# Three blocks of mm1 by seven products instead of four, in a fused retention and gelu kernel

## The chip, the core and the metric

The kernel runs on one core of one Trainium2 chip. A core has five engines that run their own instruction streams: PE (TensorE, matmuls; its weight loads are shown apart as PEld), DVE (VectorE), ACT (ScalarE), POOL (GpSimd) and SP (SyncE, which here only issues DMAs). They meet through semaphores. The metric is the device time of one execution in microseconds, taken several times. Durations are read from one further, profiled execution.

## The reference: what is computed

Retention with a decay, and then a feed-forward layer:

```
scores = q @ k^T / 8                      # 8 batches, 8 heads, 576 tokens, 64 per head
ret    = scores * gamma[h]**(i - j)       # for i >= j, else 0
x      = (ret @ v), heads side by side    # 4608 tokens x 512
h      = x @ w_in                         # mm1: 512 -> 2048
g      = gelu(h), tanh form
out    = g @ w_out                        # mm2: 2048 -> 512
```

All inputs and the output are float32. The kernel computes in float16 with float32 sums.

## The kernel before

**Units and blocks.** The tokens of a batch are cut into units of 128 (the fifth of a batch has 64), 40 units in all. Retention works by units: within a unit by masked scores, from earlier units by a decayed state. Its output goes transposed into `xT` (line 421), a ring of three blocks. The feed-forward layer works by blocks of 512 tokens, 0 to 8. mm1 gives h transposed in PSUM, gelu (ACT) moves it into `gT` (a ring of two blocks), and mm2 reads it from there. PSUM banks for mm1 and for mm2 are two each (`take`, line 426).

**Seven products.** A product of 2 x 2 blocks can be had with seven products of blocks instead of eight, with sums of blocks before and after (Winograd's form of Strassen's scheme). The kernel does so in two places.

- mm2 of 16 pairs of tiles of 128 tokens (blocks 1 to 7 whole, and half of 0 and of 8): `sum_a` (line 874) makes sums of gT, `sum_b` (852) sums of w_out once, `product` (892) is one of seven products of 8 matmuls of 256 columns, `assemble` (924) adds the parts on DVE or copies them on DVE or ACT.
- mm1 of the last blocks of tokens: `sum_w` (960) makes sums of w_in once, `sum_x` (977) four sums of a block's xT on DVE, `product_h` (984) is one of seven products of 4 matmuls for each of four groups of chunks, `part_h` (1007) copies three parts out of PSUM and adds three on DVE, `gelu_h` (1016) is the gelu of what comes of it. The sums of w_in lie in pages 9 to 20 of the 21 input pages, so from the first `sum_w` on, and for units from `LATE` (line 181) on, loads use nine pages only (`page`, line 185).

**The list of steps.** The order of all instructions is written out: `ORDER` (line 17) is a string of steps made beforehand, and the loop at line 1087 calls one small function for each. Every engine runs its part of the list in that order, so what stands on one engine behind a waiting instruction waits too. A step's letter, its function and its engine:

| step | does | engine |
|---|---|---|
| L,u,n | loads q, k or v (n = 0, 1, 2) of unit u; units 0, 2, 5, 7 are loaded two at once ("wide", 512 KB) | SP's queue |
| I,g,by / J,g,by | loads one of eight pieces of w_in / w_out; by g: POOL's queue with the cast in the transfer; by p: SP's queue as float32 into a staging slot (`load_w`, line 253) | POOL or SP |
| i,g,eng / j,g,eng | casts a staged piece; does nothing for a piece that came by g (`cast_w`, 261) | DVE, ACT or POOL |
| q, k, v | scale or cast a unit's input to float16 (lines 439 to 493) | DVE, ACT, POOL |
| t, y / D | transpose q and k: by PE and a copy / by a DMA | PE, then DVE or ACT / SP |
| X, Y, R, B | retention's matmuls of wide units / of others | PE |
| m, a, o, z, x | mask, state, its decay, its float16 copy, output to xT | DVE, ACT, POOL |
| N,t,fc,half | mm1 of block t: two chunks of 128 features, 256 tokens (8 matmuls of 256 columns, line 790) | PE |
| M,t,fc[,part] | mm1: one chunk, 512 tokens (4 matmuls of 512), or with a part four chunks, 128 tokens (16 of 128) | PE |
| F, G | gelu after N, M (line 798) | ACT |
| U / s / A / l / f | sums of w_in / sums of xT / one of the products of mm1 / copy or addition / gelu | DVE / DVE / PE / ACT, DVE / ACT |
| O, e | plain mm2, a quarter of the sum for 128 tokens (line 816); its result | PE; DVE, ACT |
| T / H / W / V | sums of w_out / sums of gT / one of the products of mm2 (line 904) / parts and results (all DVE sums and additions show as line 850) | DVE / DVE / PE / DVE, ACT |
| P, E, Q | mm2 of the last 128 tokens by columns (line 1031), result, store | PE; DVE, ACT; SP |
| S | store | SP |
| K,n | n dummy matmuls of 512 columns (line 1046) | PE |
| Z, g, c, b, w | constants: zeroed state buffers, rows of decays, mask, tables, the gelu table | POOL, DVE, ACT |

mm2 of earlier blocks and mm1 of later ones are interleaved on PE, with retention's small matmuls between them.

Of the kernel before, what the change touches and what calls it, by code (L numbers as in the profile page):

```python
# [17 lines left out]
Z,0,g L,4,1 L,0,2 L,0,1 Z,1,v g,g Z,3,v c k,0,a L,0,0 b I,6,g L,2,0 v,0,v K,4 K,4 K,4 K,4 t,0,k,h  # L18
y,0,k,v q,0,g Z,5,v X,0 I,7,g K,4 K,1 t,0,q,h I,2,g L,2,1 q,2 y,0,q,v a,0,1,g z,0,1,a I,3,g a,1,1
K,4,o K,3,o Y,0,1 L,2,2 Z,2,g L,4,0 m,0,1 k,2,a K,4 K,2 Y,0,0 m,0,0 o,1,1 t,2,k,h L,5,0 t,2,q,h  # L20
y,2,k,a R,0 L,5,1 I,1,g y,2,q,v x,1 x,0 L,4,2 I,0,g z,1,1,g K,4 Y,2,0 L,5,2 L,7,0 k,4,v v,2,v
t,4,k,o N,0,12,0 I,4,g N,0,14,0 w y,4,k,a X,2 m,2,0 a,2,1 F,0,12,0 F,0,14,0 L,7,1 a,3,1 Y,2,1 I,5,g
z,2,1,g m,2,1 N,0,6,0 N,0,4,0 F,0,4,0 q,4,g F,0,6,0 R,2 x,3 t,4,q,o x,2 N,0,0,0 N,0,2,0 q,5 y,4,q,a
v,4,g B,4,-1 F,0,0,0 m,4 Z,4,g J,1,g N,0,4,1 F,0,2,0 t,5,q,o M,0,9 y,5,q,v k,5,v v,5,v J,0,g F,0,4,1
N,0,0,1 G,0,9 J,2,g M,0,8 L,7,2 t,5,k,o z,3,1,v F,0,0,1 N,0,12,1 q,7,g G,0,8 y,5,k,a J,3,g N,0,14,1
Y,5,0 J,4,g k,7,g X,5 F,0,12,1 F,0,14,1 M,0,10 m,5,0 N,0,2,1 a,5,1,g J,7,g t,7,q,o L,9,0 a,6,1
G,0,10 B,-1,4 z,5,1,v Y,5,1 J,5,g m,5,1 M,0,11 F,0,2,1 N,0,6,1 t,7,k,o x,4 J,6,g y,7,k,v y,7,q,a R,5
O,0,4 O,0,0 o,6,1 F,0,6,1 Y,7,0 x,5 x,6 G,0,11 N,1,4,0 N,1,0,0 F,1,4,0 F,1,0,0 O,0,1 O,0,5 L,14,1
L,9,1 N,1,14,0 F,1,14,0 v,7,g H,0,1,5,v m,7,0 U,1,0 N,1,2,0 F,1,2,0 Y,7,1 X,7 L,9,2 a,7,1 z,7,1,a
N,1,10,0 O,0,6 N,1,6,0 F,1,6,0 m,7,1 q,9,g k,9,g a,8,1 z,6,1,v O,0,7 U,2,0 L,11,0 T,1,0,v e,0,1,v  # L30
H,0,1,2,v T,1,1,v R,7 v,9,g L,13,0 j,2,g F,1,10,0 D,9 T,2,1,v x,7 N,1,12,0 x,8 q,11 L,10,0 H,0,1,4,v
W,0,1,1 O,0,2 L,14,2 F,1,12,0 q,10,g L,10,1 N,1,12,1 L,11,1 F,1,12,1 T,2,0,v O,0,3 T,3,1,v B,9,-1
e,0,0,a T,4,0,v k,10,v V,0,1,0,v L,10,2 L,14,0 D,10 N,1,8,0 q,13 N,1,0,1 L,12,0 W,0,1,5 F,1,8,0
F,1,0,1 N,1,2,1 T,4,1,v N,1,14,1 F,1,2,1 L,11,2 k,11,g F,1,14,1 D,11 L,13,1 W,0,1,6 m,9 i,2,g
V,0,1,1,a N,1,8,1 T,3,0,v v,10,v j,4,g L,16,0 N,1,10,1 F,1,8,1 W,0,1,7 z,8,1,v B,10,9 V,0,1,3,a
L,12,1 x,9 m,10 V,0,1,4 N,1,4,1 W,0,1,4 F,1,10,1 a,10,0,g N,1,6,1 a,10,1 z,10,1,a W,0,1,3 v,11,g
z,10,0,v H,1,0,5,v B,11,10 V,0,1,5,v L,12,2 q,12 m,11 F,1,6,1 W,0,1,2 q,14 k,13,g a,11,0 F,1,4,1
W,1,0,1 x,10 N,2,10,0 L,15,0 V,1,0,0,a k,12,g N,2,14,0 H,1,0,2,v F,2,10,0 F,2,14,0 H,1,1,5,v V,0,1,6
V,0,1,2 v,12,v W,1,0,6 H,1,1,2,v L,16,1 j,3,v D,12 N,2,8,0 L,15,2 N,2,4,0 V,1,0,1,v L,13,2 D,13
L,15,1 a,11,1 o,11,1 z,11,0,a W,1,1,1 F,2,8,0 W,1,0,7 F,2,4,0 v,14,g B,12,11 V,1,1,0,v H,1,0,4,v  # L40
v,15,v i,5,a S,0,1 q,15,g a,12,0 z,11,1,a v,13,g i,0,a L,19,1 N,2,0,0 U,1,1 m,12 W,1,1,6 x,11 L,18,0
# [88 lines left out]
def kernel(  # L130
# [11 lines left out]
    B, H, S, D = q.shape  # L142
# [12 lines left out]
    G = 64  # L155
# [25 lines left out]
    LATE = 26  # L181
# [595 lines left out]
    gTs, h = {}, {}  # L777
# [341 lines left out]
```

## Time and profile before

| | |
|---|---|
| time, median of 3 runs | 295.02 us (294.54 to 295.3) |
| the profiled execution | 295.5 us |
| its span in the profile | 293.8 us |
| granted TensorE clock | 1.00 |
| PE, PEld, DVE, ACT, POOL busy | 280.0, 233.0, 225.7, 166.6, 95.7 us |
| matmuls of plain mm1 (L790) | 608, 79.0 us |
| matmuls of mm1 by seven products (L1001) | 192 + 128 + 64 + 64 |
| matmuls of mm2 by seven products (L904) | 384 + 256 + 128 + 128 |
| HBM read, written | 36.70 MB, 9.44 MB |

A busy PE is the time in which some matmul is in its pipeline; a single matmul of 256 columns is shown as 273 ns long, though the next one starts earlier. What one costs in a row of them is seen from the length of a group in the chain of waits. Lines in the profile name the helper that issues an instruction, so DVE's sums and additions share line 850 and are told apart by their tiles: `pages` and `hc` are those of mm1 by seven products, `ssum` and `tsum` those of mm2.

### The profile page before, as it was taken

How to read it: one execution, taken by the hardware profiler on the slowest of the kernel's cores; microseconds unless marked ns; L12 is line 12 of the kernel's file. 1: busy time of each engine (PE TensorE's matmuls, PEld its weight loads, DVE VectorE, ACT ScalarE, POOL GpSimd, SP SyncE). 2: the span in 40 equal slices, each digit the busy share in tenths (PEclk: the TensorE clock that was granted, in tenths of full speed). 3: DMA queues.
4: the chain of work that ended last, by engine and by line, in shares of the span. 5: the costliest groups of instructions: out<-in, count | busy, mean ns of one | idle time of the engine just before them, and what ended most of it. 6: DMA issues, size and time to landing. Idle time of an engine off the chain costs nothing.

```text
span 293.8 us, 9639 instructions
## 1 busy us (share of the span) xinstructions
PE 280.0 (95%) x4042; PEld 233.0 (79%) x4042; DVE 225.7 (77%) x446; ACT 166.6 (57%) x325; POOL 95.7 (33%) x157
## 2 busy tenths in 40 slices
PE   7697999999999999999999899999999999999995
PEld 2366767788888888888888778878887788888874
DVE  6684874986976798748758798899988989985841
ACT  2464763456655534656457558578576697655510
POOL 7841791202531321434643534644313301000000
PEclk9999999999999999999999999999999999999999
DMA  6999999949989979999998979997948430110112
GB/s 159 312 247 212 310 203 207 186 94 225 169 207 233 198 168 196 222 206 159 248 206 196 184 163 197 197 188 193 181 87 187 109 126 2 38 74 36 74 71 108
DMA packets 136428, 49.77 MB, mean 169 GB/s; under 512 B 118209, under 2 KB 130881, under 8 KB 136385
## 3 DMA queue, kind: packets, MB, share of 16 engines
q1 hardware_dynamic: 132032, 44.97, 70.6%
q0 software_dynamic: 4352, 4.20, 8.5%
q8 instruction: 31, 0.51, 0.8%
q14 instruction: 13, 0.10, 0.1%
HBM read 36.70 MB, written 9.44 MB: 157 GB/s over the span
## 4 chain that ended last, share of the span: by engine, by line
PE 77%; DVE 11%; DMA 5%; issue 2%; ACT 1%; SPq 1%; POOL 1%; DVEq 0%; POOLq 0%; ACTq 0%
PE bank L904 29%; PE bank L790 21%; PE bank L1001 14%; PE bank L816 4%; DMA w_in_sb<-in_moe_w_in_dram 3%; DVE ssum L850 2%; DVE pages L850 2%; PE sk L574 2%; PE x L550 2%; DMA pages<-in_q_dram 2%; PE sk L584 1%; PE x L595 1%; PE bank L1031 1%; DVE sz L764 1%; DVE hc L850 1%
## 5 line engine op out<-in xcount | busy, mean ns | idle before, releaser
L790 PE MATMUL bank<-xT,w_in_sb 128*128 128x256 f16 (+1 forms) x608 | 79.0, 279 | 1.8 <-ACT xT L607 0.9
L798 ACT ACTIVATE gT<-bank 128x512 f16<-128x512 f32 x80 | 47.0, 597 | 39.5 <-PE bank L790 39.2
L790 PEld LDWEIGHTS <-w_in_sb 128*128 128x128 f16 x608 | 57.5, 98 | 13.2 <-DMA w_in_sb<-in_moe_w_in_dram 2.5
L904 PEld LDWEIGHTS <-ssum 128*128 128x128 f16 x512 | 49.8, 98 | 6.8 <-DVE ssum L850 0.9
L904 PE MATMUL bank<-tsum,ssum 128*128 128x256 f16 x384 | 49.3, 273 | 0.3 <-DVE ssum L850 0.3
L904 PEld LDWEIGHTS <-gT 128*128 128x128 f16 x384 | 37.0, 98 | 4.4
L441 POOL TENSOR_TENSOR v<-pages,dec 128x512 f16<-128x512 f32 (+1 forms) x24 | 24.2, 1010 | 48.5 <-DMA pages<-in_v_dram 26.6
L286 POOL CAST sz<-s 64x256 f16<-64x256 f32 x36 | 17.3, 479 | 62.1 <-DVE s L746 51.6
L904 PE MATMUL bank<-w_out_sb,gT 128*128 128x256 f16 x256 | 32.9, 273 | 0.0
L1001 PEld LDWEIGHTS <-pages 128*128 128x128 f16 x256 | 24.2, 98 | 7.1 <-issue 2.9
L1001 PE MATMUL bank<-pages 128*128 128x256 f16 x192 | 27.9, 273 | 1.9 <-DVE pages L850 1.3
L722 DVE TENSOR_TENSOR ret<-sk,mask 128x512 f16<-128x512 f32 (+1 forms) x32 | 19.8, 618 | 9.8 <-PE sk L584 5.2
L850 DVE TENSOR_TENSOR ost<-u,bank 128x256 f32<-128x256 f32 x48 | 19.4, 416 | 9.5 <-PE bank L904 9.3
L850 DVE TENSOR_TENSOR ssum<-gT,ssum 128x1024 f16<-128x1024 f16 x32 | 24.0, 754 | 0.1
L284 ACT COPY hc<-bank 128x512 f32<-128x512 f32 x27 | 15.8, 586 | 14.1 <-PE bank L1001 13.8
L850 DVE TENSOR_TENSOR ssum<-gT 128x2048 f16<-128x2048 f16 (+1 forms) x20 | 21.3, 1063 | 2.7 <-ACT gT L798 2.1
L850 DVE TENSOR_TENSOR hc<-hc,bank 128x512 f32<-128x512 f32 x29 | 19.8, 684 | 4.0 <-PE bank L1001 3.8
L1001 PEld LDWEIGHTS <-w_in_sb 128*128 128x128 f16 x192 | 18.6, 98 | 2.9 <-DVE pages L850 0.6
L441 POOL TENSOR_TENSOR qk<-pages,dec 128x512 f16<-128x512 f32 (+1 forms) x16 | 17.1, 1070 | 9.7 <-DMA pages<-in_q_dram 4.8
L746 DVE TENSOR_TENSOR s<-s,sk 128x256 f32<-128x256 f32 x36 | 15.0, 416 | 5.8 <-PE sk L584 4.5
L1001 PE MATMUL bank<-xT,w_in_sb 128*128 128x256 f16 x128 | 19.2, 273 | 0.0
L1019 ACT ACTIVATE gT<-hc 128x512 f16<-128x512 f32 x29 | 17.8, 630 | 2.0 <-DVE hc L850 2.0
(117 smaller groups left out, 445.9 us busy)
## 6 DMA issues: line engine op xcount, KB each, us to landing
out_dram<-ost SPq DMA_DIRECT2D x35, 256.0 KB, 2.6
pages<-in_q_dram SPq DMA_DIRECT2D x32, 256.0 KB, 5.1
pages<-in_k_dram SPq DMA_DIRECT2D x24, 256.0 KB, 4.4
pages<-in_v_dram SPq DMA_DIRECT2D x24, 256.0 KB, 4.4
pages<-in_v_dram SPq DMA_DIRECT2D x4, 512.0 KB, 12.5
pages<-in_k_dram SPq DMA_DIRECT2D x4, 512.0 KB, 6.9
w_in_sb<-in_moe_w_in_dram POOLq DMA_DIRECT2D x8, 256.0 KB, 10.2
w_out_sb<-in_moe_w_out_dram POOLq DMA_DIRECT2D x8, 256.0 KB, 7.9
```

The source lines that it names most:

```text
L284: nc.scalar.copy(out=o, in_=i)
L286: (nc.vector if eng == "v" else nc.gpsimd).tensor_copy(out=o, in_=i)
L441: eng.tensor_tensor(out=out, in0=pages[:, page_of[s["u"], i], 0:n], in1=dec[:, i // 2, s["j"], 0:n].unsqueeze(2).to_broadcast([128, n, D]) ...
L722: nc.vector.tensor_tensor(out=ret[:, :, 0:n], in0=now["two"][:, :, 0, 0:n], in1=mask.unsqueeze(1).unsqueeze(1).to_broadcast([128, 2, n, G] ...
L746: nc.vector.tensor_tensor(out=s32, in0=state[0], in1=kv, op=ALU.add)
L790: nc.tensor.matmul(hps[:, i, :], w_in_sb[:, ct, 128 * (fc + i) : 128 * (fc + i) + 128], xT[:, ct, TB * t % XR + lo : TB * t % XR + hi], st ...
L798: nc.scalar.activation(out=gTs[t][:, fc : fc + TB // (hi - lo), lo:hi], in_=h.pop((t, fc, lo)), func=AF.Gelu_apprx_tanh, bias=0.0, scale=1.0,)
L816: nc.tensor.matmul(ops[t, tcc], gTs[t][:, ft, 128 * tcc : 128 * tcc + 128], w_out_sb[:, ft, :], start=(ft == 0), stop=(ft == NFC - 1),)
L850: (nc.vector if eng == "v" else nc.gpsimd).tensor_tensor(out=out, in0=a, in1=b, op=op)
L904: nc.tensor.matmul(p["ps", bank][:, HN * col : HN * col + HN], a[:, k], b[:, k], start=(k == 0 and fresh), stop=(k == HK - 1), skip_group_ ...
L1001: nc.tensor.matmul(p["ps", bank][:, n], w[:, c, 128 * n : 128 * n + 128], x[:, c], start=(n == 0 and c == 0 and i in (1, 2, 5)), stop=(c = ...
L1019: nc.scalar.activation(out=gTs[t][:, f : f + 2, o : o + 256], in_=p["ps", 0] if i == 0 else p["c", i], func=AF.Gelu_apprx_tanh, bias=0.0, ...
```

## The change

Only the string `ORDER` and one number are changed. The steps that differ in number or kind:

| step | before | after |
|---|---|---|
| blocks of mm1 by seven products | 5, 6, 7, 8 | 6, 7, 8 |
| A (products of mm1) | 112 | 84 |
| s (sums of xT) | 16 | 12 |
| l (copies and additions) | 96 | 72 |
| f (gelu after these) | 64 | 48 |
| N (8 matmuls of 256) | 72 | 64 |
| M of 4 matmuls of 512 / of 16 matmuls of 128 | 8 / 0 | 24 / 8 |
| F, G (gelu after these) | 72, 8 | 64, 32 |
| W (products of mm2), pairs | 112, 16 | 112, 16 |
| H (sums of gT; step 5 makes two sums at once) | 52 | 55 |
| K (dummy matmuls) | 38 | 42 |
| pieces of w_in by POOL's queue / by SP's | 8 / 0 | 7 / 1 |
| all steps | 1369 | 1336 |

Nearly every step stands at another place than before, and many of q, k, v, z, V, l and y are done by another engine: q on DVE 18 to 11 and on POOL 18 to 25, z on DVE 20 to 11, on POOL 22 to 27 and on ACT 14 to 18. `g` (rows of decays) goes from POOL to DVE. The head of the list, where w_in and w_out are loaded, and the entry into seven products:

```diff
-Z,0,g L,4,1 L,0,2 L,0,1 Z,1,v g,g Z,3,v c k,0,a L,0,0 b I,6,g L,2,0 v,0,v K,4 K,4 K,4 K,4 t,0,k,h
-y,0,k,v q,0,g Z,5,v X,0 I,7,g K,4 K,1 t,0,q,h I,2,g L,2,1 q,2 y,0,q,v a,0,1,g z,0,1,a I,3,g a,1,1
...
-v,4,g B,4,-1 F,0,0,0 m,4 Z,4,g J,1,g N,0,4,1 F,0,2,0 t,5,q,o M,0,9 y,5,q,v k,5,v v,5,v J,0,g F,0,4,1
...
-L,29,0 L,28,1 o,26,1 x,26 s,5,1 F,4,10,1 V,3,0,2,a F,4,14,1 W,3,1,2 A,5,0,1 s,5,2 W,4,0,1 L,29,1
...
+L,0,1 Z,1,v Z,5,v g Z,4,g L,0,2 L,0,0 k,0,a K,4 K,3 t,0,k,o v,0,v b q,0 I,0,g K,3 X,0 a,0,1,g a,1,1
+L,2,0 K,4 K,4 K,3 t,0,q,h y,0,k,a I,1,g c I,6,g L,2,1 z,0,1,g y,0,q,a L,2,2 q,2 L,4,0 K,4 K,1 Y,0,1
+m,0,1 L,4,1 L,5,0 K,4 K,2 Y,0,0 L,5,1 w t,2,q,h y,2,q,a k,2,v K,4 K,1 t,2,k,o m,0,0 o,1,1 y,2,k,v
+R,0 x,0 K,2 Y,2,0 M,0,0,0 x,1 Z,2,g v,2,v I,2,p Z,3,v Z,0,g I,7,g z,1,1,a q,4,g I,3,g G,0,0,0 K,1
+X,2 m,2,0 a,2,1 N,0,12,0 a,3,1 k,4,a k,5,g I,4,g t,4,k,o Y,2,1 z,2,1,a L,5,2 t,4,q,o L,7,0 N,0,14,0
+F,0,12,0 F,0,14,0 I,5,g m,2,1 R,2 y,4,k,a M,0,0,1 y,4,q,a x,2 B,4,-1 M,0,0,2 t,5,k,o x,3 q,5 L,7,1
+i,2,v m,4 t,5,q,o L,4,2 G,0,0,1 G,0,0,2 M,0,4 M,0,5 v,5,g y,5,k,v L,7,2 J,1,g q,7,g G,0,4 M,0,6
+G,0,5 N,0,12,1 y,5,q,a X,5 J,0,g Y,5,0 z,3,1,v G,0,6 m,5,0 J,3,g F,0,12,1 M,0,7 L,10,1 k,7,v G,0,7
...
+F,5,12,0 z,25,1,g a,26,1 D,27 L,31,0 N,5,0,0 H,4,0,2,v V,3,1,6,v m,26 x,25 F,5,0,0 L,30,0 v,27,g
...
+k,34,v o,31,1 m,31 s,6,3 v,32,g V,4,1,5,a W,4,1,3 A,6,0,1 V,4,1,2,a z,30,1,g L,36,1 z,31,1,g s,6,2
+W,5,0,1 L,35,1 H,5,1,3,v H,5,1,1,v l,6,0,0,a A,6,0,6 V,5,0,0,a V,4,1,6,v L,37,1 A,6,0,2 l,6,0,1,a
...
-    LATE = 26
+    LATE = 31
```

The first sum of w_in (U), from which on nine pages serve for loads, stands near unit 14's loads before and near unit 23's casts after.

More of the change, by code (lines that the diff above doesn't have):

```diff
@@ new lines @@
+W,2,0,7 H,2,1,3,v z,16,0,g G,2,8,3 a,16,1 N,3,8,0 m,16 N,3,12,0 H,2,1,1,v F,3,8,0 D,19 W,2,0,2
+B,17,16 V,2,0,3,v F,3,12,0 H,2,0,4,v o,16,1 N,3,10,0 H,2,1,2,v W,2,0,4 a,17,0 x,16 V,2,0,2,a
+z,16,1,g D,18 V,2,0,4,v L,20,1 a,17,1 m,17 L,22,1 F,3,10,0 N,3,6,0 W,2,0,3 L,21,1 z,17,0,a v,18,v
+H,2,1,4,v F,3,6,0 N,3,4,0 N,3,2,0 z,17,1,g L,21,2 V,2,0,6,v V,2,0,5,v k,21,v B,18,17 L,20,0 F,3,4,0
+F,3,2,0 W,2,1,1 a,18,0 m,18 N,3,14,0 V,2,1,0,v L,19,2 a,18,1 F,3,14,0 L,22,0 W,2,1,2 x,17 z,18,0,g
+q,22,g q,20 W,2,1,6 L,24,0 L,22,2 S,1,2 N,3,8,1 k,22,v V,2,1,1,v S,1,3 L,20,2 N,3,12,1 B,19,18
@@ new lines @@
+W,2,1,7 z,18,1,v k,20,v q,21,g W,2,1,5 F,3,8,1 D,20 N,3,6,1 L,23,0 V,2,1,3,a F,3,12,1 x,18 F,3,6,1
+W,2,1,4 N,3,0,1 H,3,0,5,v v,20,g v,19,g m,19 B,20,19 v,22,g N,3,14,1 H,3,0,2,v V,2,1,5,v V,2,1,4,v
+v,21,g W,2,1,3 W,3,0,1 F,3,0,1 V,2,1,2,a a,20,0 D,21 F,3,14,1 k,23,v x,19 U,1,0 S,2,1 N,3,4,1
+z,20,0,a m,20 N,3,2,1 V,2,1,6,v F,3,4,1 D,22 a,20,1 L,24,1 F,3,2,1 B,21,20 U,3,0 j,0,g a,21,0
+N,3,10,1 L,25,1 W,3,1,1 L,23,2 z,20,1,g q,24,g N,4,2,0 x,20 m,21 z,21,0,g V,3,0,0,a k,24,g L,27,0
+L,24,2 a,21,1 v,23,g L,27,1 W,3,0,6 F,3,10,1 N,4,12,0 F,4,2,0 S,2,0 H,3,1,5,v q,23,g U,1,1 L,26,2
@@ new lines @@
+l,7,0,2,a q,37,g A,7,0,2 m,36 k,39,a D,37 l,7,0,3,v W,6,0,5 a,36,1 o,36,1 S,5,0 f,6,3,3 A,7,0,4
+A,7,0,5 f,7,0,0 f,7,0,1 L,38,2 z,36,1,a W,6,0,6 A,7,1,1 l,7,0,4,v A,7,0,3 D,38 l,7,1,0,a l,7,0,5,v
+S,5,1 v,38,g B,37,36 A,7,1,6 V,6,0,1,a j,4,g D,39 A,7,1,2 v,39,g l,7,1,1,a W,6,0,7 m,37 a,37,0
+l,7,1,3,v a,37,1 A,7,1,7 x,36 V,6,0,3,v V,6,0,4,v l,7,1,2,a H,6,0,4,v A,7,1,5 f,7,1,1 z,37,0,g
+B,38,37 m,38 S,5,3 f,7,0,3 A,7,1,4 f,7,1,0 f,7,0,2 W,6,0,4 A,7,2,1 V,6,0,5,a l,7,1,4,v A,7,1,3
+a,38,0 H,6,1,5,v W,6,0,3 l,7,2,0,a z,38,0,g V,6,0,2,a S,5,2 A,7,2,6 l,7,1,5,v W,6,1,1 A,7,2,2
@@ new lines @@
+H,6,1,2,v l,7,2,1,a V,6,1,0,a A,7,2,7 W,6,1,6 f,7,1,3 l,7,2,3,v A,7,2,5 x,37 l,7,2,2,v A,7,2,4
+V,6,0,6,v l,7,2,4,v V,6,1,1,a f,7,2,1 a,38,1 f,7,2,0 f,7,2,2 W,6,1,7 A,7,2,3 l,7,2,5,v A,7,3,1
+W,6,1,2 i,4,a A,7,3,2 l,7,3,0,a A,7,3,6 f,7,1,2 V,6,1,3,v l,7,3,3,v W,6,1,5 l,7,3,1,v z,37,1,a
+z,38,1,g B,39,38 H,6,1,4,v V,6,1,2,a A,7,3,7 m,39 W,6,1,4 x,38 f,7,2,3 B,-1,39 l,7,3,2,v A,7,3,5
+f,7,3,1 V,6,1,4,v l,7,3,4,v A,7,3,4 x,39 f,7,3,0 V,6,1,5,a s,8,1 W,6,1,3 s,8,3 A,7,3,3 A,8,0,1 s,8,2
+l,8,0,0,a W,7,0,1 l,7,3,5,v S,6,1 V,7,0,0,a V,6,1,6,v A,8,0,6 l,8,0,1,a H,7,0,5,v s,8,4 A,8,0,2
@@ new lines @@
+W,7,0,2 A,8,0,7 H,7,0,2,v W,7,0,6 j,7,v f,7,3,3 l,8,0,3,v f,7,3,2 S,6,2 l,8,0,2,a V,7,0,1,a
+H,7,1,5,v A,8,0,4 A,8,0,5 f,8,0,0 l,8,0,4,v W,7,0,7 A,8,1,1 A,8,0,3 W,7,0,5 l,8,0,5,v l,8,1,0,a
+V,7,0,3,v A,8,1,6 A,8,1,2 l,8,1,3,v f,8,0,1 H,7,0,4,v W,7,0,4 f,8,0,3 l,8,1,1,a A,8,1,7 A,8,1,5
+V,7,0,5,a l,8,1,2,a A,8,1,4 V,7,0,4,v W,7,0,3 H,7,1,2,v S,6,3 S,6,0 f,8,1,0 l,8,1,4,v A,8,1,3
+A,8,2,1 f,8,0,2 l,8,2,0,a V,7,0,2,a f,8,1,1 W,7,1,1 l,8,1,5,v A,8,2,2 V,7,1,0,v A,8,2,6 W,7,1,6
+l,8,2,1,a l,8,2,3,v A,8,2,7 V,7,0,6,v A,8,2,5 l,8,2,2,v V,7,1,1,a f,8,1,2 W,7,1,7 H,8,0,3,v A,8,2,4
@@ L126 @@
+Q,2
 """
```

167 lines of the change are left out of this document (63 added, 104 removed).

## The prediction

> **What bounds the kernel now.** I read the stretches of the span first, then the PE's waits, then the chain of waits at the start, then the DMA issues. The page's head and four stretches:
>
> ```profile
> PE 280.0 (95%) x4042; PEld 233.0 (79%) x4042; DVE 225.7 (77%) x446; ACT 166.6 (57%) x325; POOL 95.7 (33%) x157
> ...
> 45.00:165.00 120.00, 119.74 (x1886) 102.85 (x1885) 89.85 (x170) 65.25 (x131) 39.12 (x50) 1.00 1.00 196
> 165.00:200.00 35.00, 33.21 (x505) 28.74 (x503) 31.48 (x60) 23.53 (x47) 16.18 (x24) 1.00 0.88 184
> 200.00:240.00 40.00, 38.62 (x557) 34.04 (x555) 37.46 (x72) 27.82 (x57) 10.55 (x15) 1.00 0.67 144
> 240.00:280.00 40.00, 39.47 (x442) 34.75 (x440) 31.18 (x61) 25.92 (x50) 0.79 (x2) 1.00 0.13 50
> ```
>
> Columns: stretch, length, then busy us of PE, PEld, DVE, ACT, POOL, the granted clock, DMA share, GB/s. From 45 to 165 us the PE idles 0.26 us: nothing but its work counts there. From 165, where blocks 5 to 8 take mm1 by seven products, it idles 1.79, 1.38 and 0.53 = 3.7 us, and DVE is 90 and 94% busy in the first two stretches. The PE's waits from 160 to 290 us are nearly all for DVE:
>
> ```profile
> PE bank L1001 <- DVE pages L850: 1.6, 3, 0.8
> PE bank L1001 <- DVE hc L850: 0.8, 2, 0.7
> PE bank L1001 <- ACT hc L284: 0.5, 2, 0.3
> ```
>
> Before 45 us transfers set the pace: the DMA share is 1.03 from 0 to 30 us and 1.20 from 30 to 45, and the PE fills its waits with dummy products K.
>
> **The change, part by part.** The tally used below is the list of steps, each step's instructions times the mean of their row. DVE instructions overlap a little, so its sums (246 us before) stand 9% above the busy time (225.7); I use differences and ratios only.
>
> *Products.* The chain of waits has the price of a matmul of 256 columns:
>
> ```profile
> 59.12 0.86 PE bank L816 x4
> ...
> 159.62 1.75 PE bank L790 x16
> ```
>
> 1.75 / 16 = 0.109 us. A plain block has 16 steps N of 8 such matmuls, 128; a block by seven products 4 groups x 7 x 4 = 112. Block 5 goes from 112 to 128: **+16 x 0.109 = +1.75 us**, on the engine that sets the end, with no cover. M steps of 512 columns (4 matmuls, as in the four of L816 above, 0.86) cost what an N costs. Eight M steps now take 128 columns (16 matmuls). Nearest row: in the tail L1031 does 16 of 256 and 16 of 128 columns in 2.80 us, so 16 of 128 take at most 2.80 - 1.75 = 1.05 with the pipeline's end in it; 0.87 to 1.05 against 0.87, for eight 0 to +1.4. I take 0, since most of the difference is that end.
>
> *What leaves DVE.* Block 5 no longer needs 4 sums s of xT (4 x 0.60 = 2.4), 12 additions l (12 x 0.684 = 8.2) nor 12 copies l (mostly ACT's, 12 x 0.586 = 7.0). By choice of engine in the new list z loses 8.8 on DVE and q 4.5, k and v gain 3.2. In all the tally gives DVE -17.7, ACT -8.4, POOL +9.3 us. None of that is the end by itself; it counts only through the PE's 3.7 us of waits. Those split so. The two waits where block 5's sums come in (168.66 us: 0.77, and 171.09: 0.37, both for "DVE pages L850") are the price of entering seven products; block 6 now enters first, so I keep them. The other 0.65 of the stretch 165 to 200 goes with block 5. For the 1.38 and 0.53 of blocks 6 to 8, compare equal work: from the first sum of block 6 to the first of block 8 the old list has 59.7 us of DVE steps to 57.0 of PE, the new one 55.8 to 56.5. DVE is relieved by 6.5% there, not more, because nearly all that left is block 5's own. I take 0.55 of these 1.9 as gone. **-1.2 us**, between -0.65 (only block 5's own) and -3.5 (all waits).
>
> At the entry, one rule speaks against the change:
>
> ```profile
> 167.34 1.26 DVE L850 TENSOR_TENSOR pages<-xT 128x512 f16<-128x512 f16 x1
> ...
> 167.13 1.19 POOL L441 TENSOR_TENSOR v<-pages,dec 128x512 f16<-128x512 f32 x1 [2.08 <-DMA pages<-in_v_dram]
> ```
>
> The sum of xT took 1.26 us beside POOL's product; the shortest of the eight took 0.41. The Trainium skill, page "SBUF — State Buffer", section "Who interferes with whom", says that a DVE instruction with two inputs in SBUF contends with a GpSimd instruction that reads SBUF. By that rule, which these two lines agree with, POOL's 9.3 us more of work take back part of DVE's relief; with the relief of blocks 6 to 8 gone, -1.2 becomes -0.65 and the sum is higher by 0.55.
>
> *The start.* The old list reads w_in by POOL's queue alone, from 8.25 us; the new one issues pieces 0 and 1 right after the first memset on POOL (about 4.7) and piece 2 by SP, behind the loads of units 0 and 2 and of q and k of units 4 and 5. The bytes stay the same. What the PE meets last there is w_out: the first mm2 step of the list reads pieces 0 and 1 of it, and in the old list POOL issued them behind v of unit 4:
>
> ```profile
> 30.96 0.61 POOL L441 TENSOR_TENSOR v<-pages,dec 128x256 f16<-128x256 f32 x1 [6.66 <-DMA pages<-in_v_dram]
> 31.98 2.36 POOL L255 DMA_DIRECT2D w_out_sb<-in_moe_w_out_dram  x3
> 34.35 1.92 POOL L457 TENSOR_TENSOR wide<-pages,decw 128x1024 f16<-128x1024 f32 x1
> ...
> 42.76 1.47 PE L816 MATMUL bank<-w_out_sb,gT 128*128 128x512 f16 x6
> ...
> pages<-in_v_dram SPq DMA_DIRECT2D x1, 512.0 KB, 16.2
> ...
> w_out_sb<-in_moe_w_out_dram POOLq DMA_DIRECT2D x2, 256.0 KB, 6.6
> ```
>
> In the new list piece 1 of w_out stands on POOL behind v of unit 5, and piece 0 behind q of unit 7 as well. Unit 5's v was issued at 16.2 and landed 16.2 us later, at 32.4; ahead of it and with it went 4.9 MiB by SP (units 0, 2, 4, 5) and the 4 MiB of w_in. In the new list it is 5.25 (piece 2 is in it, one load of unit 4 is not) and 3.5: the same sum, so it lands at about 32.3. POOL then scales it (1.92, row L457): 34.2; issues piece 1 (0.7): 34.9; scales q of unit 7 (1.92; its last half landed 6.6 us after 27.2): 36.8; issues piece 0. With the 6.6 us of the two issues shown it lands at 43.4, with the 7.9 of all eight at 44.7. The old list began mm2 at 42.76; the new one has 0.4 us more PE work ahead of it by the tally, so 43.2 on the same pace. **+0.6 us**, between +0.2 and +1.5 by these rows; and whatever the earlier pieces of w_in win before that, this wait takes back. If the first 10 us (215 GB/s, against 267 in the next ten) carry the difference, 0.5 MB, all of it lands 1.7 us earlier: -1.1. If piece 2 is starved (below): +2.0.
>
> *Covered edits.* 42 dummy products instead of 38: 4 x 0.217 = 0.9, in the waits of the first 15 us; +0.9 if these are gone. The cast of piece 2 (as L286's cast of 1024 columns, 0.68) on DVE, which idles 10 of the first 30 us. gseg's memsets go from POOL (1.45) to DVE. Sums of w_in (U) come at units 23 to 30 instead of 14 to 25 and all 21 pages serve longer, so loads go out earlier; from 45 to 165 there is 0.26 us to win. Nearly all of 1,336 steps stand elsewhere, and a new wait there has no room: 0 to +1.5; I take 0, as the old list shows that such an order can be kept almost without waits.
>
> **Sum.** 1.75 - 1.2 + 0.6 = +1.15 us on the profiled execution (295.5 us, span 293.8 and 1.7 around it, unchanged): 296.65. The median of the three runs is 295.02, 0.48 lower: **296.2 us**.
>
> **The rivals.**
> 1. *DVE stops setting the PE's pace* (faster). If the waits of blocks 6 to 8 come from a backlog that block 5 builds up on DVE (94% busy from 200 to 240), it never forms and 3.3 of the 3.7 go; the pieces of w_out come 0.6 earlier than on the old pace. 1.75 - 3.3 - 0.6 = -2.15: 292.9. For it: the releasers are DVE, and DVE falls below the PE's work (55.8 to 56.5). Against: each wait ends with one sum or one addition, and relief per block is small. It decides once more waits go than the products cost: over 1.75 us of them with an even start, over 2.35 with the start of the forecast.
> 2. *A wash.* Half of the waits go (-1.8) and the start is even: -0.05, 295.0.
> 3. *Piece 2 is starved* (slower still). While three and more pieces of w_in were queued, SP's k of unit 5, issued at 13.1, took 14.4 us, and the 64 KB of unit 4's v behind it 15.4. Piece 2 stands just there. If it lands at 31 and not at 27 to 28, the fifth mm1 step (M of chunk 4) starts after the cast, at 31.7; the new list has 11.3 us of PE work before it, which the old PE had done by 29.7. +2.0 in place of +0.6: 297.6. Against: POOL's last two pieces now wait behind k of unit 5, so SP has the engines to itself then.
>
> That the change doesn't do what it says can be excluded: the list is the program.
>
> **How the numbers follow.** Forecast 0.38, rival 1 0.33, rival 2 0.20, rival 3 0.09. A measurement here tells about 0.3%, 0.9 us, from no change: faster 0.33, same 0.20, slower 0.38 + 0.09 = 0.47. The range takes in rival 1 and its edge (1.75 - 3.3 - 0.9) and rival 3 with a 1.4 us of quarter steps or new waits on top: 292.6 to 299.0; outside lies what both gains or all losses at once give. The slower cases alone span 296.0 to 299.0.
>
> **What would show it.** Matmuls of L1001 fall from 448 to 336 and L790 rises: right if the PE's busy time without K grows by about 1.7. PE idle from block 6's first sum to 280 us: about 2.5 by the forecast, under 1 by rival 1. The first L816: after 43.2 and released by a w_out transfer by the forecast; at 41 to 42 in rival 1. A PE wait of over 2 us on the cast of w_in before the first 512-column M is rival 3. Wrong altogether if the PE has waits of more than 1 us between 45 and 165, or a mean granted clock below 1.00.

## The result, and the profile after

The changed kernel takes 297.42 us (median of 5 runs, 296.53 to 297.89) where the kernel before takes 295.02 (5 runs, 294.54 to 295.30): a ratio of 1.0076, 95% interval 1.0054 to 1.0098. Ratios here leave out a run that is over 1.5% above the fastest of its kernel. It is slower, by 0.8%, and the time lies in the forecast's range, 1.2 us above its value. The way there was another one than the forecast's, though: two of its terms came out better than written, and a loss that it had put at nothing was the largest of all.

Its profiled execution took 297.42 us, with a span of 295.7 and a mean granted clock of 0.994. Line numbers are 3 lower than before (L790 is L787, L904 is L901, L1001 is L998, L816 is L813, L850 is L847) and 5 more lower in the experiments made from it. The page's head, and the stretches that answer to those of before:

```profile
PE 282.9 (96%) x4062; PEld 230.4 (78%) x4062; DVE 211.9 (72%) x427; ACT 159.6 (54%) x314; POOL 114.0 (39%) x162
...
PEclk9999999999999999999997999999999999999999
```

```profile
20.00:30.00 10.00, 9.82 (x180) 7.39 (x178) 7.89 (x10) 6.78 (x15) 5.80 (x6) 1.00 1.15 310
30.00:45.00 15.00, 15.00 (x240) 9.91 (x241) 9.55 (x12) 8.21 (x16) 11.44 (x14) 1.00 1.23 226
45.00:165.00 120.00, 116.69 (x1807) 98.05 (x1796) 80.48 (x154) 59.65 (x119) 46.67 (x58) 0.99 0.99 188
165.00:200.00 35.00, 33.76 (x486) 27.08 (x484) 28.38 (x53) 19.80 (x41) 21.02 (x23) 1.00 1.01 191
200.00:240.00 40.00, 39.40 (x664) 35.07 (x662) 34.24 (x69) 28.39 (x59) 13.36 (x21) 1.00 0.74 154
240.00:280.00 40.00, 39.63 (x396) 35.00 (x395) 30.24 (x55) 25.92 (x52) 3.12 (x4) 1.00 0.13 51
```

Read the second column, PE busy, against the length. From 45 to 165 us, where the old kernel idled 0.26, the new one idles 3.31, and the clock is 0.99. From 200 to 280 us it idles 0.97, where the old one idled 1.91. The PE's waits after 45 us:

```profile
PE sk L581 <- DMA qkT<-qk: 3.0, 2, 2.7
PE sk L571 <- DVE ret L719: 1.2, 1, 1.2
PE bank L998 <- ACT gT L1016: 0.6, 1, 0.6
```

No wait for a sum of xT or for "hc" is left; instead there are two for retention, and they stand here in the PE's own timeline (start, length, instruction, idle time before it and its releaser):

```profile
155.00 0.32 PE L571 MATMUL sk<-v,qk 64*64 64x64 f16 x16
158.04 0.32 PE L581 MATMUL sk<-qkT 64*64 64x64 f16 x16 [2.72 <-DMA qkT<-qk]
158.19 0.23 PE L592 MATMUL x<-ret,v 64*64 64x64 f16 x8
158.35 1.38 PE L787 MATMUL bank<-xT,w_in_sb 128*128 128x256 f16 x8
159.53 1.91 PE L901 MATMUL bank<-w_out_sb,gT 128*128 128x256 f16 x8
...
171.11 0.32 PE L571 MATMUL sk<-v,qk 64*64 64x64 f16 x16 [1.24 <-DVE ret L719]
```

The first wait is step B,25,24 waiting for the transposed q and k of unit 25 (step D,25). After it eight matmuls of L901 take 1.91 us; the same group takes 1.04 elsewhere. The stretches around show why: the clock.

```profile
150.00:158.00 8.00, 5.32 (x84) 3.85 (x82) 3.79 (x6) 2.65 (x5) 2.69 (x3) 1.00 0.95 145
158.00:163.00 5.00, 4.96 (x46) 3.16 (x47) 2.10 (x6) 1.40 (x4) 0.00 (x0) 0.66 1.11 258
163.00:171.00 8.00, 6.88 (x112) 5.79 (x109) 7.96 (x13) 3.92 (x7) 6.12 (x6) 1.00 1.02 214
```

For 5 us the granted clock is 0.66 in the mean (0.50 in each whole microsecond from 159 to 162), which costs 5.0 x 0.34 = 1.7 us. Then DVE, busy for only 2.10 of those 5 us, is busy for 7.96 of 8 us, and the wait of 1.24 us for its masked scores follows at 171. That this second wait comes from the first is not shown: from 165 to 175 us the old kernel has DVE busy for 9.59 of 10 us too and idles 1.14 on PE, and the swap below, with a shorter first wait and a full clock, still has 1.2 us here.

To place gains and losses I count, for each stretch, the time not covered by the list's matmuls at their full price (0.217 us for 512 columns, 0.109 for 256; the price of retention's small ones is an estimate in proportion; dummy products are left out):

| stretch, us | lost before | lost after | difference |
|---|---|---|---|
| 0 to 45 | 20.0 | 18.1 | -1.9 |
| 45 to 140 | 2.8 | 3.2 | +0.4 |
| 140 to 175 | 2.3 | 6.6 | +4.3 |
| 175 to 200 | 1.7 | 0.6 | -1.1 |
| 200 to 280 | 4.4 | 3.1 | -1.3 |
| more products (16 x 0.109) | | | +1.75 |

Together +2.2; the last 14 us give 0.3 back, and the span grew by 1.9. What the change was to pay for itself with is there, 4.3 us of it. The 140 to 175 us stretch takes it all. The table has one execution of each kernel; in a second one of the changed kernel (further below) the first mm2 begins at 42.43 us and not at 41.22, so the gain at the start is known to about 1 us only.

### The profile page after: what moved, and what is told of

The parts are those of the page before. It is cut to its first block, busy times and chain, and to the rows that moved or that the text cites. A ratio compares the mean times of both kernels' runs of the same rounds, so it can differ in the third digit from the quotient of the medians.

```text
span 295.7 us, 9635 instructions
## 1 busy us (share of the span) xinstructions
PE 282.9 (96%) x4062; PEld 230.4 (78%) x4062; DVE 211.9 (72%) x427; ACT 159.6 (54%) x314; POOL 114.0 (39%) x162
## 4 chain that ended last, share of the span: by engine, by line
PE 82%; DMA 5%; DVE 5%; SPq 3%; ACT 2%; issue 1%; DVEq 0%; ACTq 0%
PE bank L901 30%; PE bank L787 25%; PE bank L998 12%; DMA qkT<-qk 4%; PE bank L813 4%; PE bank L1043 2%; DMA pages<-in_v_dram 2%; PE sk L571 2%; PE x L547 1%; PE sk L581 1%; PE bank L511 1%; PE bank L1028 1%; PE x L592 1%; SPq L229 1%; SPq L235 1%
## 5 line engine op out<-in xcount | busy, mean ns | idle before, releaser
L787 PE MATMUL bank<-xT,w_in_sb 128*128 128x256 f16 (+2 forms) x736 | 96.3, 279 | 0.2
L795 ACT ACTIVATE gT<-bank 128x512 f16<-128x512 f32 x96 | 57.0, 598 | 58.3 <-PE bank L787 56.7
L787 PEld LDWEIGHTS <-w_in_sb 128*128 128x128 f16 x736 | 65.7, 98 | 16.4 <-issue 1.0
L901 PEld LDWEIGHTS <-ssum 128*128 128x128 f16 x512 | 49.4, 98 | 7.6 <-issue 0.2
L901 PE MATMUL bank<-tsum,ssum 128*128 128x256 f16 x384 | 48.7, 273 | 0.0
L901 PEld LDWEIGHTS <-gT 128*128 128x128 f16 x384 | 37.8, 99 | 5.6
L438 POOL TENSOR_TENSOR qk<-pages,dec 128x512 f16<-128x512 f32 (+1 forms) x24 | 24.9, 1047 | 29.8 <-DMA pages<-in_q_dram 24.5
L901 PE MATMUL bank<-w_out_sb,gT 128*128 128x256 f16 x256 | 33.7, 277 | 0.0
L847 DVE TENSOR_TENSOR ost<-u,bank 128x256 f32<-128x256 f32 x48 | 19.6, 415 | 11.9 <-PE bank L901 11.0
L847 DVE TENSOR_TENSOR ssum<-gT,ssum 128x1024 f16<-128x1024 f16 x32 | 25.3, 789 | 0.1
L847 DVE TENSOR_TENSOR ssum<-gT 128x1024 f16<-128x1024 f16 (+1 forms) x23 | 20.9, 919 | 3.7 <-ACT gT L795 3.3
L998 PE MATMUL bank<-pages 128*128 128x256 f16 x144 | 20.8, 273 | 0.0
L998 PEld LDWEIGHTS <-pages 128*128 128x128 f16 x192 | 18.2, 98 | 2.4
L847 DVE TENSOR_TENSOR hc<-hc,bank 128x512 f32<-128x512 f32 x21 | 14.4, 685 | 6.4 <-PE bank L998 5.6
L611 ACT ACTIVATE xT<-x 128x512 f16<-128x512 f32 (+1 forms) x25 | 14.4, 580 | 5.7 <-PE x L592 5.5
L901 PE MATMUL bank<-w_out_sb,ssum 128*128 128x256 f16 x128 | 16.6, 273 | 0.1
L901 PE MATMUL bank<-tsum,gT 128*128 128x256 f16 x128 | 16.6, 273 | 0.0
L281 ACT COPY u<-bank 128x256 f32<-128x256 f32 x28 | 10.4, 372 | 11.4 <-PE bank L901 10.8
```

The lines of the kernel that those rows point to most:

```text
L281: nc.scalar.copy(out=o, in_=i)
L438: eng.tensor_tensor(out=out, in0=pages[:, page_of[s["u"], i], 0:n], in1=dec[:, i // 2, s["j"], 0:n].unsqueeze(2).to_broadcast([128, n, D]) ...
L611: nc.scalar.activation(out=xT[:, :, o : o + G * (b - a)].rearrange("c p (h s) -> c p h s", s=G), in_=x[:, a:b].rearrange("c h p s -> c p h ...
L787: nc.tensor.matmul(hps[:, i, :], w_in_sb[:, ct, 128 * (fc + i) : 128 * (fc + i) + 128], xT[:, ct, TB * t % XR + lo : TB * t % XR + hi], st ...
L795: nc.scalar.activation(out=gTs[t][:, fc : fc + TB // (hi - lo), lo:hi], in_=h.pop((t, fc, lo)), func=AF.Gelu_apprx_tanh, bias=0.0, scale=1.0,)
L847: (nc.vector if eng == "v" else nc.gpsimd).tensor_tensor(out=out, in0=a, in1=b, op=op)
```

## The experiments

Theories to tell apart. **A**: the loss is one late operand, the transpose of unit 25, with the drop of the clock and the backlog that it leaves; the rest of the change is a small gain. **Rivals**: an earlier wait of SP is the root (C); VectorE or GpSimd is simply too full there; or the trade of products against waits was bad in itself. A letter in a quoted expectation means what that text says of it. Every series has runs of the kernel before next to it; its runs lie between 293.5 and 297.9 us there, so a single profiled execution can be some 2 us off its median, and the ratios with their intervals decide.

**The transpose of unit 25 earlier.** Edit of the list:

```diff
-D,24 x,22 q,26,g M,4,5 H,3,0,4,v
+D,24 x,22 k,25,v D,25 q,26,g M,4,5 H,3,0,4,v
...
-v,25,v k,25,v v,26,v M,4,7 G,4,5 D,25 G,4,7
+v,25,v v,26,v M,4,7 G,4,5 G,4,7
```

> The new list with two steps of unit 25 moved ahead: the cast of k before unit 29's load of v, and the transpose D right behind it, so that SP issues it some 2.5 us earlier. Theory A, the loss of the new list is one transpose that comes late: the PE stood 2.7 us for it at 158 us, then had a granted clock near 0.5 for some 3 us (about 1.5 us lost), then stood 1.2 us at 171 for a mask that was late on DVE. With the transpose landed by 154 us all three go or shrink: 297.4 - 3.5 to 5, so 292.5 to 294. Theory B, all loads and transposes are late there, so the next one takes its place: at most 1 us less, 296.4 to 297.4.

Measured: 294.96 us (10 runs), ratio to before 0.9966 (0.9940 to 0.9992). The clock is 1.00 in the profiled execution, and what waits remain in this stretch are short:

```profile
PE sk L566 <- POOL v L433: 0.7, 1, 0.7
PE bank L993 <- DVE pages L842: 0.6, 1, 0.6
PE sk L566 <- DVE s L738: 0.5, 1, 0.5
PE sk L576 <- DMA qkT<-qk: 0.3, 1, 0.3
```

Two steps moved among 1,336 turn the change's loss into a small gain, as theory A has it and B does not. The time is 1 us above A's own 292.5 to 294, so the gain is smaller than A had said.

**Only its data earlier, not its place in SP's queue.**

```diff
-v,25,v k,25,v v,26,v
+k,25,v v,25,v v,26,v
```

> The changed kernel with one swap: VectorE scales k of unit 25 before v of unit 25; the transpose D,25 stays at its place in the list. Theory A1 (the transpose was late because of its place in SP's queue, behind a load and a write of the result: k was ready at 151.18 us, the transpose issued at 152.06): the swap makes k ready earlier but the transpose is issued when it was, so the wait of 2.7 us at 158 us stays (2 to 3 us), and the time stays within 0.5 us of the changed kernel's 297.4. Theory A2 (it was late because of its data, the k that VectorE made last): the wait falls by about 1 us or more and the time is 295 to 296.5.

Measured: 296.45 us (10 runs), ratio 1.0021 (1.0003 to 1.0040). The profile decides more than the time. In the changed kernel DVE's cast of k of unit 25 ends at 151.18 us, SP issues the transpose at 152.06, and it lands at 158.00, 5.9 us later. With the swap that cast ends at 150.75; the transpose is issued at 152.56 and lands at 158.40, 5.8 us later. SP, in the changed kernel:

```profile
148.17 1.29 SPq L501 DMA_TRANSPOSE qkT<-qk  x1
149.56 1.26 SPq L235 DMA_DIRECT2D pages<-in_v_dram  x2
150.87 0.61 SPq L805 DMA_DIRECT2D out_dram<-ost  x1
151.58 0.37 SPq L229 DMA_DIRECT2D pages<-in_v_dram  x1
152.06 3.69 SPq L501 DMA_TRANSPOSE qkT<-qk  x2
```

Between the transposes of units 24 and 25 stand three loads and a store of the result. The one issued before them (148.17) landed in 2.5 us, the one behind them in 5.9; in the version above, right behind unit 24's, it took 3.1, and there the transpose of unit 26, which then stood first behind the same three loads and store, took 5.7 (4.3 in the changed kernel). So it is its place in SP's queue that makes it late (A1), and the data only a little. The wait fell from 2.7 to 1.6 us all the same, because PE itself came there 1.5 us later, and in this profiled execution the clock stayed full at that wait. The shorter wait and the time are thus what A2 had expected (295 to 296.5, where A1 had 297.4 within 0.5), but A2's reason is not: with its data ready 0.4 us earlier the transpose was issued 0.5 us later.

**SP not held at the transpose of unit 23.**

```diff
-S,2,0 H,3,1,5,v q,23,g U,1,1
+S,2,0 H,3,1,5,v q,23 U,1,1
```

> The new list with one word changed: q of unit 23 is scaled on DVE and not on POOL. SP stood at unit 23's transpose from 135.5 to 138.8 us until POOL had scaled that q, with six loads of units 25 and 26 and two transposes behind it. Theory C, that is the root of the later wait: SP goes on at about 135.5, everything behind it comes 2 to 3 us earlier, the PE's wait at 158 us falls under 1 us and the clock stays at 1: 293 to 295. Theory A (only unit 25's own transpose is placed too late, its k waits behind a v on DVE): the wait stays within 1 us of 2.7: 296.4 to 297.4.

Measured: 295.71 us (10 runs), ratio 1.0001 (0.9971 to 1.0031). SP issues unit 23's transpose at 138.82, as before (138.79), so this edit did not free SP, and C as the root was not put to its test; but the first experiment takes the loss away with SP held as long (139.28). The time lies between the two expectations. The waits are still there, 2.1 us for the transpose at 158.3 and 1.9 us for DVE at 170.5, and yet it is faster than the changed kernel: its clock was 1.00 in nine runs of ten and 0.999 in the tenth. That points to the clock as a part of the loss by itself.

**The change undone in part: block 5 plain in the old list.** In the list of before, block 5's steps s, A, l and f are replaced by N and F in their places:

```diff
-x,26 s,5,1 F,4,10,1 V,3,0,2,a F,4,14,1 W,3,1,2 A,5,0,1 s,5,2 W,4,0,1 L,29,1 l,5,0,0,a V,3,1,6,v
+x,26 F,4,10,1 V,3,0,2,a F,4,14,1 W,3,1,2 N,5,0,0 W,4,0,1 L,29,1 V,3,1,6,v
...
```

> The list of before, with block 5 alone made plain in its place: each group of seven products becomes four N steps with their gelus, its copies, additions and sums of xT are left out, nothing else is moved. It tells what one block by seven products is worth when the list stays. Forecast of the prediction: +1.75 for the products, -1.2 for waits, so 0.55 over before, ratio 1.002. DVE sets the pace (rival 1): waits of 3 us go, 0.995. If no waits go at all: 1.006.

Measured: 295.41 us (12 runs), ratio 0.9988 (0.9967 to 1.0009): a wash, and none of the three values expected lies in the interval. Its stretches, to be held against those of before:

```profile
165.00:200.00 35.00, 34.92 (x526) 31.05 (x524) 23.20 (x46) 18.52 (x38) 18.05 (x24) 1.00 0.93 194
200.00:240.00 40.00, 38.75 (x558) 34.12 (x557) 36.30 (x71) 27.99 (x57) 9.43 (x14) 1.00 0.68 142
240.00:280.00 40.00, 39.47 (x442) 34.74 (x441) 32.12 (x61) 25.50 (x49) 0.79 (x2) 1.00 0.11 41
```

From 165 to 200 us the old list idled 1.79; this one 0.08. So with block 5 plain, both its own waits and the two at the entry (0.77 and 0.37), which the forecast had handed on to block 6, are gone; the 1.25 and 0.53 of blocks 6 to 8 remain nearly whole (1.38 and 0.53 before), so there was no backlog that block 5 built up for them. What goes (1.8 us by these rows) is what the products cost (1.75): the exchange of block 5 by itself is even.

**The start: pieces of w_in earlier on POOL.**

```diff
-q,4,g I,3,g G,0,0,0 K,1 X,2 m,2,0 a,2,1 N,0,12,0 a,3,1 k,4,a k,5,g I,4,g
+I,3,g I,4,g I,5,g q,4,g G,0,0,0 K,1 X,2 m,2,0 a,2,1 N,0,12,0 a,3,1 k,4,a k,5,g
...
-F,0,14,0 I,5,g m,2,1
+F,0,14,0 m,2,1
```

> The new list with the last three pieces of w_in issued by POOL before it scales q of unit 4 and casts k of unit 5, and not behind them. By the ledger of the prediction all 3.5 MiB are then ahead of v of unit 5, which lands at about 32 us and not at 28; the first pieces of w_out are issued some 4 us later and the first mm2 step starts at 43 to 45 us and not at 41: time 2 to 4 us over that of the new list, 299.4 to 301.4. Rival: the PE is not held by w_out at the start, and has its w_in earlier: within 0.7 us of the new list.

Measured: 299.09 us (4 runs), ratio 1.0119 (1.0072 to 1.0166), just under what was expected. The interval overlaps with the changed kernel's (1.0054 to 1.0098), so the trace has to decide. In the changed kernel POOL's products for units 4 and 5 hold pieces 4 and 5 back:

```profile
20.02 0.76 POOL L252 DMA_DIRECT2D w_in_sb<-in_moe_w_in_dram  x1
23.87 1.81 POOL L283 CAST wide<-pages 128x1024 f16<-128x1024 f32 x1 [3.10 <-DMA pages<-in_k_dram]
25.63 1.46 POOL L252 DMA_DIRECT2D w_in_sb<-in_moe_w_in_dram  x2
28.19 2.08 POOL L454 TENSOR_TENSOR wide<-pages,decw 128x1024 f16<-128x1024 f32 x1 [1.10 <-DVE qkT L283]
30.22 0.76 POOL L252 DMA_DIRECT2D w_out_sb<-in_moe_w_out_dram  x1
```

They are issued at 25.6 and 26.4 us, when v of unit 5, issued at 18.6, is nearly there (28.02). With the three pieces ahead of these products, v of unit 5 lands at 30.97, PE waits 1.7 us for the cast of unit 5's k, and the first mm2 begins at 43.84 instead of 41.22 (42.43 in the changed kernel's second execution). So 1.4 to 2.6 us of the start were won by the order of the transfers, and the units' inputs are what it waits for.

**The start: piece 2 by POOL as the others.**

```diff
-v,2,v I,2,p Z,3,v
+v,2,v I,2,g Z,3,v
```

> The changed kernel with piece 2 of w_in issued by POOL's queue as the other pieces, not by SP with a landing buffer and a cast: same place in the list. Theory A (the start was gained by the place of pieces 3 to 5 behind the q and k of units 4 and 5 on POOL, not by the other queue): v of unit 5 lands within 1 us of 28.0, the first mm2 begins at 41 to 42 us, and the time is within 1 us of the changed kernel's 297.4. Rival (the other queue is what gained it, since POOL issues one piece less): the first mm2 begins 1 to 2 us later and the time is 298.4 to 299.4.

Measured: 297.06 us (10 runs), ratio 1.0037 (1.0009 to 1.0064). v of unit 5 lands at 27.9 and the time is no longer than the changed kernel's, as A has it; but the first mm2 begins at 42.34, not before 42, and PE waits 1.0 us for a piece of w_in there. In the changed kernel it begins at 41.22 us in one profiled execution and at 42.43 in the other, so this one execution does not tell what the other queue is worth, and the times don't show it.

**A version that takes the next wait away too.** The transpose as in the first experiment, and the load of v of unit 27, which landed at 166.5 us and held POOL and then PE (the 0.7 above), three loads earlier:

```diff
-x,23 W,3,1,5 L,28,0 V,3,0,6,v
+x,23 W,3,1,5 L,27,2 L,28,0 V,3,0,6,v
...
-G,4,10 G,4,11 L,27,2 B,26,25
+G,4,10 G,4,11 B,26,25
```

> The changed kernel with k of unit 25 and its transpose moved ahead (as in e2_k25_d25), and with the load of v of unit 27 issued three loads earlier on SP, ahead of q of unit 28. In e2_k25_d25 that v landed at 166.5 us and PE waited 0.7 us for POOL's scaling of it at 167.6. If the rest is a matter of single late operands as theory A says: that wait goes, 0.3 to 0.7 us off e2's ratio of 0.9966, so 0.994 to 0.996 of the kernel before. If VectorE or POOL are simply full here (rival): the wait reappears at another tile and the ratio stays at 0.996 to 0.998.

Measured: 295.03 us (12 runs), ratio 0.9972 (0.9946 to 0.9998). The wait for POOL's v is gone, but a wait of 0.5 us for DVE's masked scores has come. Both this and the ratio are what the rival had said (0.996 to 0.998), not theory A (0.994 to 0.996): the transpose was one late operand, and what is left behind it is not. With the next edit added (q of unit 23 by DVE, `q,23` for `q,23,g`):

> e7_l27 and also q of unit 23 scaled by VectorE instead of POOL, so that SP is not held at the transpose of unit 23. Theory C as a second, independent cause (SP held there makes the loads behind it late): 0.3 to 1 us below e7_l27. Rival (it made no difference alone, and VectorE gains 0.8 us of work in a stretch where it is nearly full): within 0.4 us of e7_l27 or up to 0.8 us slower.

Measured: 295.17 us (12 runs), ratio 0.9976 (0.9953 to 1.0000): no different, as the rival has it. SP issues unit 23's transpose at 138.41 here and at 139.59 without this edit, so SP was freed by little, and C finds no support as a second cause.

**The changed kernel and that version in one series.** No edit in the first; the second is the version with both moves.

> The changed kernel itself, unaltered, so that it stands in one series with the next two. By all theories a ratio of 1.005 to 1.010 to the kernel before. By the theory of the clock, runs in which the granted clock is below 1.00 have a span 0.8 to 2 us above runs in which it is 1.00.

> The kernel of e7_l27 again, beside the changed kernel: a ratio to the kernel before of 0.994 to 0.998, so 2.0 to 4.0 us less than e9_after. If the change's loss were not in the one late transpose and the clock behind it (rival), the two would be within 1 us.

Measured: 297.66 us (7 runs), ratio 1.0049 (1.0018 to 1.0079), and 294.36 (12 runs), ratio 0.9967 (0.9942 to 0.9991): the medians differ by 3.3 us. The version beats both kernels. Its stretch, and that of the changed kernel in this series:

```profile
140.00:175.00 35.00, 33.95 (x524) 26.27 (x522) 27.35 (x53) 19.20 (x42) 15.54 (x16) 1.00 1.00 185
```

```profile
140.00:175.00 35.00, 31.81 (x450) 24.28 (x449) 24.74 (x46) 16.61 (x36) 13.12 (x16) 0.95 0.95 186
```

2.1 us of idle time and 0.05 x 35 = 1.75 us of clock lie between the two. The seven runs of the changed kernel bear the second figure out: four with a mean clock of 0.993 or 0.994 have a span of 295.9 to 296.5, three with 0.998 or 1.00 one of 293.8 to 295.3, a difference of the medians of 1.8 us. The mean clock alone does not say where a drop lies or what it costs, though: six of the 82 runs of the kernel before in the three series show 0.994 too, with a median span of 293.1 against 293.8 of the others. In the changed kernel eight of the twelve runs here show 0.994 or less, with the transpose of unit 25 moved ahead (the first experiment and both series of this version) seven of 34.

**The transpose later still.**

```diff
-G,4,5 D,25 G,4,7
+G,4,5 G,4,7
...
-F,4,12,1 D,26 B,24,23
+F,4,12,1 D,26 D,25 B,24,23
```

> The changed kernel with the transpose of unit 25 issued one place later on SP, behind that of unit 26. Theory A (PE waits for this one transpose): it lands 0.5 to 1 us later, PE's wait at 158 us grows from 2.7 to 3.2 to 4 us, and the time is 0.5 to 1.3 us above the changed kernel's in the same series. Theory of the clock: with a wait over 3 us the clock falls to half in every run, again for 3 to 4 us, so that the mean granted clock is 0.994 in all of them. Rival (the wait is only where a shortage of VectorE shows): the same time, the next wait at 171 us shorter by as much.

Measured: 299.36 us (4 runs, 296.88 to 301.47), ratio 1.0107 (1.0064 to 1.0150). The transpose lands 0.9 us later (160.06 for 159.18), as A has it, and the median is 1.7 us above the changed kernel's in this series, more than expected; but it rests on four runs, and the intervals of the two ratios overlap. In its profiled execution, the slowest of the four, the wait was 2.6 us, 0.2 more, not over 3, since PE came later as well; the clock fell in three of four runs, not in all. Of the two claims the later landing holds, the price of it is not settled, and the one on the clock wasn't put to its test, for want of the longer wait.

## Why the prediction was right in its range and wrong in its reasons

*Products.* +1.75 us, as written: 336 matmuls of L998 instead of 448. The M steps of 128 columns: 1.07 us in the trace with the pipeline's end, where the same step by 512 columns shows 1.04; 0, as taken.

*The start*, **wrong**: forecast +0.6, measured -1.9 in the profiled execution, outside its bounds (-1.1); in the second execution the first mm2 begins at 42.43, still before the forecast's 43.2. The step that failed is "the same sum, so it lands at about 32.3": v of unit 5 landed at 28.02. Two things in it were off. Pieces 4 and 5 of w_in stand behind k of unit 5 on POOL and were issued at 25.6 and 26.4, so they were not ahead of that v; the prediction had seen this place of the two pieces (it uses it against rival 3) and not taken them out of its sum. And the rate was taken as given: from 20 to 30 us the transfers moved 310 GB/s instead of 220, at nearly the same busy share (1.15 and 1.20). The moved pieces are tested by the fifth experiment; why the rate was higher was not tried by itself. Piece 2 of w_in landed 7.3 us after its issue, at 25.19, so rival 3 fell.

*The stalls of seven products*, **wrong in size**: forecast -1.2, measured -2.4 in the two last rows of the table, and more if the old kernel's entry waits before 175 are counted. The step that failed is "block 6 now enters first, so I keep them": from 190 to 200 us, where block 6 enters, PE doesn't wait at all. Its first two sums of xT end at 196.7 and 198.2, 0.41 us each, with DVE 83% busy. PE doesn't wait there in the version with both moves either; the first experiment's profile has one wait of 0.6 us for a sum. From block 6's entry to 280 us 0.97 us are idle, near rival 1's "under 1" and far from the forecast's 2.5. For blocks 6 to 8 the forecast's own split (0.55 of 1.9 gone) was less wrong: 0.94 went. By the undone experiment nearly nothing of that comes from block 5 itself; in the changed kernel it comes with the rest of the new list.

The rule of the Trainium skill on DVE and GpSimd ("SBUF — State Buffer", "Who interferes with whom") would have taken back part of this relief. At block 6's entry nothing of it is to be seen: the sum at 196.27 had no POOL instruction beside it, the one at 197.75 had a POOL cast beside it (197.35 to 198.42), and both took 0.41 us. In the lost stretch it is not plain either: beside POOL's three products of 148.4 to 151.6 us two products v on DVE, each with two inputs, took 0.74 and 1.10 us, where the mean of that form is 0.76. The change in the sum that I had put beside the rule, 0.55 us, was in any case smaller than the error of the term.

*New waits in the remade list*, **wrong, and it decided**: forecast 0 (0 to +1.5), measured 2.7 and 1.24 us of waits and 1.7 of clock, 5.6 in all, some 4.3 net of what the old list lost there; the version with both moves, in one series with the changed kernel, is 3.3 us shorter. The step that failed is "I take 0, as the old list shows that such an order can be kept almost without waits". That the old list keeps it says nothing about the new one: the new list could be read, and in it three loads and a store stand between D,24 and D,25 on SP, with B,25,24 to come. The prediction named this as its own refutation (waits over 1 us between 45 and 165, a clock below 1.00), and both came.

So the forecast of a slower kernel was right by luck: by a loss that it had not counted. Without that loss, rival 1 was nearer in its signs: mm2 at 41.2, no waits at the entry. Its mechanism, a backlog that block 5 builds up for blocks 6 to 8, is not borne out: with block 5 plain in the old list their waits stayed (1.25 and 0.53 us). What in the new list shortens them stays open. With the transpose mended the kernel is 0.3% faster than before (ratios 0.9966, 0.9972 and 0.9967), not rival 1's 0.7% (292.9 us): about 1 us of gain where rival 1 had 2.15.

## What to carry to other kernels

When a list of steps is made anew, read each engine's queue at the places where the order is tight, above all what stands between two transposes on the queue that also loads and stores: one operand that came 2.7 us late cost here, with what followed, 2.4 to 3.3 us by the ratios and medians above, more than one block by seven products saves (1.75 us). A wait on PE has a second price, the clock: look at the granted clock behind each wait of 2 us or more before you count the wait alone. And a sum of bytes ahead of a transfer holds only for what is issued ahead of it, so follow each issue to the instruction it stands behind.

## What the runs showed of the hardware

**The clock falls after a short idle time.** In four of the profiled executions above with a PE gap of 2.2 to 2.9 us near 158 to 160 us (start to start, less one step), and in that of w_in first (2.35), the granted clock is 0.50 for 3.41 us, beginning 0 to 1.5 us after PE has resumed; with a gap of 1.8 us (the swap) and one of 2.3 (q of unit 23 by DVE) it stays at 1.00. What tells them apart is where the gap lies. In all 13 profiled executions the clock changes only at whole multiples of 3.41 us from its first record, which is where the full clock begins (5.32 us in the changed kernel; the fall at 158.92 comes 45 such steps later). How busy PE was in the step just before decides. Three such steps: the one before the fall in the changed kernel, the one before the fall in its second execution, and the emptiest of the run with q of unit 23 by DVE, after which the clock stayed full:

```profile
155.51:158.92 3.41, 0.88 (x30) 0.78 (x31) 0.50 (x1) 0.00 (x0) 1.04 (x1) 1.00 1.29 178
```

```profile
157.31:160.72 3.41, 1.49 (x35) 1.34 (x36) 0.69 (x1) 0.32 (x2) 0.61 (x1) 1.00 1.03 161
```

```profile
167.19:170.60 3.41, 1.53 (x35) 1.30 (x37) 3.37 (x7) 1.19 (x2) 1.75 (x3) 1.00 1.34 232
```

Of all such steps within the 13 spans, the six with PE busy for 1.41 us or less were each followed by a fall, of two with 1.5 us one was, and of over 1,000 with 1.53 us or more none. The gap of 2.3 us that brought no fall lies across two steps, with PE busy for 2.7 and 2.0 us. So here a gap of 2 us or so can bring the fall if it lies within one step, and where the steps lie differs from one execution to the next. The Trainium skill, "TensorE: Matmul & The Clock Gate", section "What's actually happening", puts the fall after an idle window of about 3.4 us that runs freely, and the return after as long a busy one. The length of the window and its running freely agree with these figures; that the window has to be idle does not, as PE was busy for up to 1.5 us of it.

**The clock column misses the start.** It counts from that first record on. Before it, dummy products of 512 columns start 0.43 us apart, behind it 0.22, while the column shows 1.00 for both. The record lies between 5.1 and 10.7 us in these executions, at 5.32 and 10.54 in the two of the changed kernel, whose first mm2 begin at 41.22 and 42.43; whether the one brings the other was not tried.

**A transpose's time depends on what the queue holds.** In the changed kernel the 31 transposes by DMA landed 2.4 to 6.0 us after their issue; the one that decided took 5.9 behind three loads and a store, and 3.1 when it was moved right behind another transpose. The next one, then first behind those loads and the store, took 5.7.
